# Column 0 of h in the second half: from twelve plain products per token tile to the rounds of seven block products

## The chip, the cores and the metric

The kernel runs on one core of one Trainium2 chip. The metric is the device time of one execution in microseconds (us); lower is better. TensorE (PE in the profile; PEld is its weight loading) multiplies, VectorE (DVE) and ScalarE (ACT) work elementwise, and nearly all transfers are issued one after the other on SyncE's DMA queue (SP, SPq).

## The reference

```python
def _A_ref(x, w_r, w_i):                     # x: 2048 tokens x 576
    X = rfft2(x, axes=(-2, -1)) * (w_r + 1j * w_i)
    return irfft2(X, s=(S, D), axes=(-2, -1))

def _B_ref(x, w_gate, w_up, w_down):         # F = 4608
    h = sigmoid(x @ w_gate) * (x @ w_up)     # 2048 x 4608
    return h @ w_down                        # 2048 x 576

xn = layernorm(x)
return x + _A_ref(xn, A_w_r, A_w_i) + _B_ref(xn, B_w_gate, B_w_up, B_w_down)
```

All is float32. The kernel keeps that accuracy by splitting each factor into a high and a low part in TensorE's rounded format, so that one product of two numbers becomes three passes (high x high, high x low, low x high).

## The kernel before

**Halves, units, columns.** The 2048 tokens are done in two halves of 1024 (p = 0, 1), each as two chunks of 512 (c = 0, 1). The 4608 columns of h come in 36 blocks of 128. Unit u = 36p + f computes block f of h for the half p. Its matmuls into the banks pA, pB and pE (L710) are 128x512, seven to a product. The first two units of a half are "plain" (four products per chunk), all others are made of seven block products, that is 49 matmuls; product 0 of a unit is put already among the products of the unit before. ScalarE and VectorE make h from the banks (L803 to L836). Two units make a column j of h, 18 columns to a half.

**h times w_down, in two ways.** `down` (L840, matmuls at L860) takes one column and one tile of 128 tokens: 2 units x 3 passes x 2 halves of the output = 12 matmuls of 128x288 into po, then one addition to acc (L869). Eight tiles make a half, so a column costs 96 matmuls. `seven` (matmuls at L1071, bank ps) takes two columns and the whole half at once, as a 2x2 block product in seven items (`ITEMS`, `ROUND`): each item needs one sum of blocks of h (`factor`: the sum at L985, split into high and low on ScalarE at L989 and VectorE at L992) and one sum of blocks of w_down (for example T1 = B12 - B11), and has two steps of 12 matmuls of 128x288, each followed by one addition at L1005. A pair of columns costs 7 x 2 x 12 = 168 matmuls, a column alone 84. `seven` starts in the unit after the first pair is complete and makes one step behind each product of the units (`next(rounds)` in `beside`). In a "slow" pair the low part of the next item is made at its second step, otherwise at its first.

**Which columns go which way.** `SEVEN` holds columns 1 to 15. The first half pairs 2 to 15 (column 1 is done by `down`); the second half pairs [1,2], [3,4] ... [13,14] and does 15 alone. Columns 0, 16 and 17 go by `down` in both halves. `pend` holds the calls of `down` that are due, `spots` says behind which product of a unit one is put; those of column 0 of the second half lie in units 38 and 39.

**The weights of the second half.** In the first half the split blocks of w_gate and w_up go to DRAM (wsp) and come back in the second as 320 KB pieces (`get_w`, L323), seven pairs of pieces to a unit. The sums of w_down for the rounds lie in DRAM as fsp, split; an item of the second half loads its own from there (L968). The sums of the first half's pairs are made on the fly (`load_raw_d`, `sums_d` and `sub_d` at L930, `split_item` at L941). Column 1, paired only in the second half, has its sums made in the opening by `make_t` (L363). Column 0's split rows go to DRAM in the opening (wdsp) and are loaded once more for the second half (`load_rows_of`, L911).

**The middle.** The half ends with `down` for columns 16 and 17. As each tile of column 17 is added (L869), its acc is stored (`spill`, L872), and right behind that store `new_acc(1, m)` loads the rows of x that start the acc of the second half (L395). All these stand in program order on the one SP queue, so an issue that waits for its data holds those behind it. From unit 39 on the Fourier part of the result ("phase 1b", tiles 0 to 15; L502 to L543) is mixed into the units by a list of steps: its first matmul group is pd0 (L527, with cf, fh, fl), made from xs by eo (L510, L511), fh (L514, ScalarE) and fl (L515).

Of the kernel before, what the change touches and what calls it, by code (L numbers as in the profile page):

```python
# [13 lines left out]
OP = mybir.AluOpType  # L14
# [22 lines left out]
LATE = 2 * G  # L37
SEVEN = range(1, NF // G - 2)

TWOS = ([list(SEVEN[i:i + 2]) for i in range(1, len(SEVEN), 2)], [list(SEVEN[i:i + 2]) for i in range(0, len(SEVEN), 2)])  # L40
SLOTS = 10
# [122 lines left out]
def spectral_glu_kernel(ctx: ExitStack, tc: tile.TileContext, x, xt, xg, ri, w_in, w_down, out):  # L164
# [3 lines left out]
    def f32(ap):  # L168
        return ap.bitcast(F32)
# [173 lines left out]
    def parts_d(f):  # L343
        j, g = divmod(f, G)
        st, w = STD[j][:, g], flat(new_f((0, j, g), f"wd{f}"))
        placed(nc.scalar.activation(w[:, 0], st, AF.Copy))
        yield
        nc.vector.tensor_tensor(w[:, 1], st, f32(w[:, 0]), op=OP.subtract)
        if j not in SEVEN:
            nc.sync.dma_start(wdsp[f], f32(w).rearrange("p a d -> p (a d)"))  # L350
        else:
            for b in range(2):
                if (g, b) != (0, 1):
                    nc.sync.dma_start(fsp[j][:, WHERE[f"B{g + 1}{b + 1}"]], f32(w[:, :, b * HD:(b + 1) * HD]))
        yield

    def make_d(f, n):
# [3 lines left out]
        yield from parts_d(f)  # L361

    def make_t(j):  # L363

        b = STD[j].rearrange("p g (b d) -> p (g b) d", b=2)
        t = R["pool"].tile([P, 4, HD], F32, tag="xa", name=f"wt{j}", bufs=TPC)
        nc.vector.tensor_tensor(t[:, 1:3], b[:, 1::2], b[:, :2], op=OP.subtract)
        yield
        nc.vector.tensor_tensor(t[:, 3], b[:, 3], t[:, 1], op=OP.subtract)
        nc.vector.tensor_tensor(t[:, 0], b[:, 2], t[:, 3], op=OP.subtract)  # L370
        yield
        th, tl = (R["pool"].tile([P, 4, HD], F32R, tag="xa", name=f"{k}{j}", bufs=TPC) for k in ("wth", "wtl"))
        nc.scalar.activation(th, t, AF.Copy)
        yield
        nc.vector.tensor_tensor(tl, t, f32(th), op=OP.subtract)
        for i, v in enumerate((th, tl)):
            nc.sync.dma_start(fsp[j][:, WHERE["T4"]:WHERE["T4"] + 4, i], f32(v))
        yield

    def make_dt(j):  # L380

        yield
        yield
        for g in range(G):
            load_d(G * j + g)
        for _ in range(3):
            yield
        for g in range(G):
            yield from parts_d(G * j + g)
        if j in SEVEN:  # L390
            yield from make_t(j)

# [338 lines left out]
    def plain_ends(u, c, G_, bank):  # L731
        ends.append(lambda: nc.vector.tensor_tensor(place(u, c), G_, bank[1], op=OP.mult))
        ends.extend(parting(u, c))

# [108 lines left out]
    def down(p, j, m, together=True):  # L843
# [18 lines left out]
        def add():  # L862
            a = acc[t].rearrange("p (b d) -> p b d", b=2)
            if not together:
                for b in range(2):
                    nc.vector.tensor_tensor(a[:, b], a[:, b], pd[b], op=OP.add)
                    (nc.sync, nc.scalar)[b].dma_start(out[t, :, b * HD:(b + 1) * HD], a[:, b])
                return
            nc.vector.tensor_tensor(a, a, po[:, :, :HD], op=OP.add)  # L869
            if j == NF // G - 1:  # L870
                if p == 0:
                    nc.sync.dma_start(spill[m * P:(m + 1) * P, :], acc[t])  # L872
                    new_acc(1, m)
                else:
                    for i in range(2):
                        (nc.sync, nc.scalar)[i].dma_start(out[t, i * N1:(i + 1) * N1], acc[t][i * N1:(i + 1) * N1, :])
# [48 lines left out]
    def d(js, nm):  # L925
        return DT["d"][:, :len(js), POS[js[0], nm]]
# [27 lines left out]
    def split_rows(j, g):  # L954
# [6 lines left out]
        nc.vector.tensor_tensor(w[:, 1], src, f32(w[:, 0]), op=OP.subtract)  # L961
        nc.sync.dma_start(wdsp[G * j + g].rearrange("p (a b d) -> p a b d", a=2, b=2), f32(w))

    def load_item(n):
# [50 lines left out]
    def seven(p):  # L1015
# [8 lines left out]

        last = TWOS[p][-1] if p == 0 else TWOS[p][-2]
        if p == 0:
# [33 lines left out]
        for i, (n, mm) in enumerate(steps):  # L1060
# [6 lines left out]
            for s in range(2):  # L1067
                m = slice((2 * mm + s) * P, (2 * mm + s + 1) * P)
                parts_ = [(g, a, b) for g in range(len(js)) for a, b in ((0, 0), (0, 1), (1, 0))]
                for q, (g, a, b) in enumerate(parts_):  # L1070
                    nc.tensor.matmul(pd[:, s], h[:, g, a, m], w[:, g, b], start=q == 0 and not seeded,  # L1071
                                     stop=q == len(parts_) - 1, skip_group_check=seeded)
            slow = len(js) == 2 and js is not last
            if mm == 0:
# [339 lines left out]
    for e, p in ((NF, 0), (LAST, 1)):  # L1414
        j = NF // G - 2
        rows = load_rows_of if p else lambda p, j, g: split_rows(j, g)
        for u, i, *todo in ((e - 3, 5, (rows, p, j, 0)) if p else (e - 2, -1, (rows, p, j, 0)),
# [8 lines left out]
            extra.setdefault((u, i), []).extend(lambda a=a: a[0](*a[1:]) for a in todo)  # L1426

    def turn(n):

# [14 lines left out]
    for p in range(PAIRS):  # L1444

        calls = [(0, 0), (1, 0), (0, 1), (1, 1)] if p == 0 else [(0, 0), (0, 1), (1, 0), (1, 1)]
        for n, (f, c) in enumerate(calls):
            u = p * NF + f
            if p == 0 and n == 2:
                sides += [make_d(0, 2), make_d(1, 2)]  # L1450
            elif p and n == 2:
                for g in range(G):
                    load_rows_of(1, 0, g)
            if p == 0 and n < 2:
# [29 lines left out]
        late_input[0] = False  # L1484
        pend = [(p, 0, m) for m in range(0 if p else TPC, TPP)]

        for f in range(G, NF):
# [15 lines left out]
            spots = {i: 1 for i in (range(5) if f % G else range(4, 7))}  # L1503
            if u == NF + G:

                spots = {3: 2, 4: 2, 5: 2, 6: 2}
            elif f == NF - 2:
                spots = {i: 1 for i in range(2, 7)}
# [74 lines left out]
```

## Time and profile before

| | |
|---|---|
| three runs, median (lowest to highest) | 1371.35 us (1370.74 to 1372.51) |
| the profiled execution: its time; its span | 1371.23 us; 1369.4 us |
| PE busy | 1356.5 us, 99% of the span, 7656 matmuls |
| PEld busy | 1200.8 us, 88% |
| DVE, ACT busy | 1068.6 us (78%), 775.5 us (57%) |
| moved by DMA | 346.56 MB, mean 253 GB/s |
| granted TensorE clock | 1.000 |

The span runs from the first to the last instruction on the core; the profiled execution's time lies 1.83 us above it. Busy times overlap, since the engines work at the same time. TensorE's matmuls are pipelined, so a single one's duration (391 ns for 128x512) is longer than the distance to the next; groups in the timeline show the distance. In the windows the columns are us, then busy time and count of PE, PEld, DVE, ACT and POOL, the granted clock, the share of the 16 DMA engines and GB/s.

### The profile page before, as it was taken

Reading aid. Unit: us, or ns where it says so; the run is one execution under the profiler, and the core shown is the slowest. Engines: PE = TensorE matmul, PEld = TensorE weight load, DVE = VectorE, ACT = ScalarE, POOL = GpSimd, SP = SyncE. Lnnn points to the kernel's source line nnn. Section 1 sums busy time; section 2 is a strip of 40 time slices with the busy share of each in tenths; the row PEclk is TensorE's granted clock in tenths of the full one; section 3 lists DMA queues with packets and bytes.
Section 4 is the critical chain, followed back from the end, with each engine's and each line's share of the span. In section 5 each row is a group of like instructions: output and inputs, shape, how many; then the busy total and the mean of one; then the engine's idle time right before and its main releaser. Section 6 shows DMA issues by size and latency. Waiting matters only on the chain.

```text
span 1369.4 us, 20371 instructions
## 1 busy us (share of the span) xinstructions
PE 1356.5 (99%) x7656; PEld 1200.8 (88%) x7656; DVE 1068.6 (78%) x1555; ACT 775.5 (57%) x1228; POOL 3.3 (0%) x5
## 2 busy tenths in 40 slices
PE   8999999999999999999999999999999999999998
PEld 6888888888888888988888998988888888899887
DVE  7978988887878787999458768668777847777886
ACT  6644667676777677843236545447767634443432
POOL 0000000000000000000000000000000000000000
PEclk9999999999999999999999999999999999999999
DMA  7567877767676776595878877799899787775643
GB/s 259 209 227 279 302 291 267 275 265 271 265 267 263 277 264 261 213 312 182 295 247 263 272 244 251 215 312 307 299 314 304 243 285 247 232 235 175 200 147 87
DMA packets 127058, 346.56 MB, mean 253 GB/s; under 512 B 12816, under 2 KB 34096, under 8 KB 122224
## 3 DMA queue, kind: packets, MB, share of 16 engines
q1 hardware_dynamic: 125968, 343.94, 72.5%
q8 instruction: 61, 1.00, 0.3%
q10 hardware_dynamic: 992, 1.31, 0.3%
q14 instruction: 37, 0.30, 0.1%
HBM read 208.74 MB, written 136.46 MB: 252 GB/s over the span
## 4 chain that ended last, share of the span: by engine, by line
PE 92%; DVE 5%; DMA 1%; ACT 1%; issue 1%; SPq 0%; ACTq 0%
PE pB L710 24%; PE ps L1071 23%; PE pE L710 16%; PE pA L710 16%; PE po L860 5%; PE pd L527 2%; PE pe L650 1%; PE pc L591 1%; PE py L619 1%; PE pa L543 1%; DMA w<-wsp 1%; PE pb L566 1%; PE pz L632 0%; DVE acc L869 0%; DVE X L1359 0%
## 5 line engine op out<-in xcount | busy, mean ns | idle before, releaser
L710 PE MATMUL pB<-X,w 128*128 128x512 f32 x1484 | 374.7, 391 | 0.1
L1071 PE MATMUL ps<-wf,hs 128*128 128x288 f32 x2436 | 358.4, 295 | 0.9 <-DVE ev L655 0.9
L1071 PEld LDWEIGHTS ps<-wf,hs 128*128 128x128 f32 x2436 | 341.7, 188 | 15.4 <-ACT u L593 1.9
L710 PEld LDWEIGHTS pB<-X,w 128*128 128x128 f32 x1484 | 270.9, 188 | 49.2 <-DVE X L477 0.6
L710 PE MATMUL pE<-X,w 128*128 128x512 f32 x1064 | 265.3, 391 | 1.7 <-DVE ys L834 1.0
L710 PE MATMUL pA<-X,w 128*128 128x512 f32 (+1 forms) x1006 | 252.8, 389 | 0.7 <-DVE X L1359 0.3
L710 PEld LDWEIGHTS pE<-X,w 128*128 128x128 f32 x1064 | 194.1, 188 | 37.9 <-issue 1.4
L710 PEld LDWEIGHTS pA<-X,w 128*128 128x128 f32 x1006 | 182.5, 188 | 33.7 <-ACT X L476 0.7
L992 DVE TENSOR_TENSOR hs<-ys,hs 128x1024 fp32r<-128x1024 f32 (+1 forms) x105 | 124.7, 1187 | 36.3 <-ACT hs L989 35.0
L989 ACT ACTIVATE hs<-ys 128x1024 fp32r<-128x1024 f32 (+1 forms) x105 | 108.0, 1029 | 42.8 <-PE ps L1071 27.0
L282 ACT ACTIVATE w<-raw 128x768 fp32r<-128x768 f32 (+1 forms) x106 | 100.2, 948 | 25.7 <-DVE raw L306 8.6
L803 ACT ACTIVATE v<-pB 128x512 f32<-128x512 f32 x68 | 40.6, 596 | 79.9 <-PE pB L710 79.4
L836 DVE TENSOR_TENSOR ys<-ys,g 128x1024 f32<-128x1024 f32 x67 | 81.9, 1223 | 3.4 <-DVE ys L834 0.5
L284 DVE TENSOR_TENSOR w<-raw,w 128x512 fp32r<-128x512 f32 (+1 forms) x106 | 81.7, 771 | 2.9 <-ACT w L282 2.8
L817 ACT ACTIVATE g<-pB 128x512 f32<-128x512 f32 x68 | 40.7, 598 | 67.3 <-PE pB L710 67.0
L985 DVE TENSOR_TENSOR ys<-ys 128x1024 f32<-128x1024 f32 (+1 forms) x60 | 71.1, 1186 | 0.7
L860 PEld LDWEIGHTS po<-wb,hp 128*128 128x128 f32 x468 | 65.2, 188 | 3.0 <-DVE acc L869 0.4
L814 DVE TENSOR_TENSOR ys<-v,pE 128x512 f32<-128x512 f32 x68 | 46.5, 684 | 27.0 <-ACT v L809 26.6
L860 PE MATMUL po<-wb,hp 128*128 128x288 f32 x468 | 67.5, 296 | 0.0
L1005 DVE TENSOR_TENSOR acc<-acc,ps 128x576 f32<-128x576 f32 x55 | 41.3, 751 | 30.9 <-PE ps L1071 30.4
L834 DVE TENSOR_TENSOR ys<-v,pE 128x512 f32<-128x512 f32 x67 | 45.9, 685 | 22.8 <-PE pE L710 21.7
L869 DVE TENSOR_TENSOR acc<-acc,po 128x576 f32<-128x576 f32 x55 | 41.1, 751 | 24.4 <-PE po L860 24.2
(185 smaller groups left out, 1581.5 us busy)
## 6 DMA issues: line engine op xcount, KB each, us to landing
w<-wsp SPq DMA_DIRECT2D x246, 320.0 KB, 4.0
wsp<-w SPq DMA_DIRECT2D x34, 2240.0 KB, 6.8
wf<-fsp SPq DMA_DIRECT2D x105, 288.0 KB, 4.2
fsp<-wf SPq DMA_DIRECT2D x98, 288.0 KB, 3.5
raw<-in_w SPq DMA_DIRECT2D x34, 768.0 KB, 6.5
x<-sc SPq DMA_DIRECT2D x16, 580.0 KB, 5.4
ri<-in_ri SPq DMA_DIRECT2D x16, 580.0 KB, 5.8
dt<-in_wd SPq DMA_DIRECT2D x32, 288.0 KB, 5.1
```

The costliest lines, as they stand in the source:

```text
L282: placed(nc.scalar.activation(o[:, :, :3, :], src, AF.Copy))
L284: placed(nc.vector.tensor_tensor(o[:, :, 3:, :], src[:, :, :KT, :], f32(o[:, :, :KT, :]), op=OP.subtract))
L710: strictly(nc.tensor.matmul(bank[:, cols], w[:, sw, :], X[:, x, sx, cols], start=start and j == 0, stop=stop and j == len(steps) - 1, skip ...
L814: nc.vector.tensor_tensor(y1, v[:, 1], bank["E"], op=OP.add)
L834: nc.vector.tensor_tensor(place(u, 0), v[:, 0], bank["E"], op=OP.add)
L836: nc.vector.tensor_tensor(h, h, g, op=OP.mult)
L860: nc.tensor.matmul(pd[b], l, r, start=start, stop=stop)
L985: nc.vector.tensor_tensor(o, at(a), at(b), op=op)
L989: nc.scalar.activation(hs[:, :, 0], o, AF.Copy)
L992: nc.vector.tensor_tensor(hs[:, :, 1], o, f32(hs[:, :, 0]), op=OP.subtract)
L1005: nc.vector.tensor_tensor(o, a, b, op=op)
L1071: nc.tensor.matmul(pd[:, s], h[:, g, a, m], w[:, g, b], start=q == 0 and not seeded, stop=q == len(parts_) - 1, skip_group_check=seeded)
```

## The change

`SEVEN` begins with column 0. The first half's pairs stay [2,3] to [14,15]; the second half's become [0,1], [2,3] ... [14,15], eight full pairs and no single column. So in the second half column 0 is no longer done by `down`: its h isn't split on its own, its rows of w_down aren't loaded for it, and units 38 and 39 have no `down` in them. The rounds begin in unit 39 in place of unit 41.

The sums of w_down for the pair [0,1] (T1 to T4 of both columns) are made by a new generator, `first_sums`, which makes one move per product of the second half's plain units, from unit 37 on: four loads of 288 KB, four subtractions, four splits on ScalarE and VectorE, eight stores of 288 KB into fsp. `make_t`, which did this for column 1 in the opening, is gone. Column 0's split blocks B11, B21, B22 go into fsp in the opening, three stores of 288 KB in place of two of 576 KB. `new_acc(1, m)` moves from behind the spills to units 38 (m = 0 to 6) and 39 (m = 7).

```diff
-SEVEN = range(1, NF // G - 2)
-
-TWOS = ([list(SEVEN[i:i + 2]) for i in range(1, len(SEVEN), 2)], [list(SEVEN[i:i + 2]) for i in range(0, len(SEVEN), 2)])
+SEVEN = range(NF // G - 2)
+
+PAIRED = [list(SEVEN[i:i + 2]) for i in range(0, len(SEVEN), 2)]
+TWOS = (PAIRED[1:], PAIRED)
...
-    def make_t(j):
...
-        nc.vector.tensor_tensor(t[:, 1:3], b[:, 1::2], b[:, :2], op=OP.subtract)
...
-        nc.vector.tensor_tensor(t[:, 3], b[:, 3], t[:, 1], op=OP.subtract)
-        nc.vector.tensor_tensor(t[:, 0], b[:, 2], t[:, 3], op=OP.subtract)
...
-        nc.scalar.activation(th, t, AF.Copy)
...
-        nc.vector.tensor_tensor(tl, t, f32(th), op=OP.subtract)
-        for i, v in enumerate((th, tl)):
-            nc.sync.dma_start(fsp[j][:, WHERE["T4"]:WHERE["T4"] + 4, i], f32(v))
...
-        if j in SEVEN:
-            yield from make_t(j)
...
-        ends.extend(parting(u, c))
+        if u < NF:
+            ends.extend(parting(u, c))
...
                     nc.sync.dma_start(spill[m * P:(m + 1) * P, :], acc[t])
-                    new_acc(1, m)
...
+    def first_sums():
+
+        js = TWOS[1][0]
+        for _ in range(4):
+            yield
+        for g in range(G):
+            load_raw_d(js, g)
+            yield
+        yield
+        yield
+        for i in range(2):
+            sums_d(js, i)
+            yield
+        sub_d(js, "T4", "B21", "T2", "B11")
+        for nm in ("T4", "T1", "T3", "T2"):
+            w = new_f((1, nm), f"wt_{nm}")
+            nc.scalar.activation(w[:, :, 0], d(js, nm), AF.Copy)
+            nc.vector.tensor_tensor(w[:, :, 1], d(js, nm), f32(w[:, :, 0]), op=OP.subtract)
+            for i, j in enumerate(js):
+                nc.sync.dma_start(fsp[j][:, WHERE[nm]], f32(w[:, i]))
+            yield
...
-        last = TWOS[p][-1] if p == 0 else TWOS[p][-2]
+        last = TWOS[p][-1]
...
-            slow = len(js) == 2 and js is not last
+            slow = js is not last
...
+    for m in range(TPP):
+        extra.setdefault((NF + G + m // 7, m % 7), []).append(lambda m=m: new_acc(1, m))
...
             elif p and n == 2:
-                for g in range(G):
-                    load_rows_of(1, 0, g)
+                sides.append(first_sums())
...
-        pend = [(p, 0, m) for m in range(0 if p else TPC, TPP)]
+        assert not (p and pend)
+        pend = [] if p else [(p, 0, m) for m in range(TPC, TPP)]
...
-            if u == NF + G:
-
-                spots = {3: 2, 4: 2, 5: 2, 6: 2}
-            elif f == NF - 2:
+            if f == NF - 2:
```

In the changed file the lines between about 350 and 960 stand some 21 lower in number (L710 is L689 there, L860 is L840, L869 is L849).

**SP's queue in the middle.** Before, from the last spills to the first pieces of unit 39's weights (w38 is the buffer of units 38 and later, wsp2 and wsp3 the stored weights of units 38 and 39):

```order
L872 DMA spill_72<-acc_163 128x576 x3
L395 DMA acc_163<-in_x 128x576 x3
L911 DMA wb1_0_0_6040<-wdsp0_109 128x1152
L911 DMA wb1_0_1_6042<-wdsp1_110 128x1152
L323 DMA w38_6055<-wsp2_75 128x640 x6
L323 DMA w38_6055<-wsp3_76 128x640
L172 DMA cf_6353<-c_cf 128x2900
L323 DMA w38_6055<-wsp3_76 128x640 x4
L502 DMA xs0_6364<-in_xt 128x768
```

And now:

```order
L852 DMA spill_72<-acc_164 128x576
L324 DMA w38_6032<-wsp2_75 128x640 x4
L374 DMA acc_164<-in_x 128x576 x5
L324 DMA w38_6032<-wsp3_76 128x640
L964 DMA fsp0_145<-wt_T4_6168 128x576
L324 DMA w38_6032<-wsp3_76 128x640
L964 DMA fsp1_146<-wt_T4_6168 128x576
L324 DMA w38_6032<-wsp3_76 128x640 x2
L964 DMA fsp0_145<-wt_T1_6183 128x576
L964 DMA fsp1_146<-wt_T1_6183 128x576
```

Unit 38's pieces moved from behind the last acc loads and the two wb loads to between and right behind the spills, five acc loads moved behind them, the wb loads are gone, and stores of the new sums stand between the pieces of unit 39. The queue then goes on:

```order
L324 DMA w38_6032<-wsp3_76 128x640
L173 DMA cf_6247<-c_cf 128x2900
L324 DMA w38_6032<-wsp4_77 128x640
L481 DMA xs0_6258<-in_xt 128x768
L173 DMA am0_6260<-c_am 128x512
L324 DMA w38_6032<-wsp4_77 128x640 x4
```

Unit 40's first pieces (wsp4) stand behind all eight stores, the 1450 KB load of cf, xs0 and am0.

**TensorE, units 38 to 40.** Before, behind the last product into pA38:

```order
L710 MATMUL pA38_6143<-X_66,w38_6055 128x512 x7
L710 MATMUL pB38_6151<-X_66,w38_6055 128x512 x7
L860 MATMUL po0_8_6195<-wb1_0_0_6040,hp1_0_0_5951 128x288 x6
L860 MATMUL po0_8_6195<-wb1_0_1_6042,hp1_0_0_5951 128x288 x6
L860 MATMUL po0_9_6208<-wb1_0_0_6040,hp1_0_0_5951 128x288 x6
L860 MATMUL po0_9_6208<-wb1_0_1_6042,hp1_0_0_5951 128x288 x6
L710 MATMUL pA39_6224<-X_66,w38_6055 128x512 x7
```

And now, from the same place up to the first group of phase 1b:

```order
L689 MATMUL pB38_6127<-X_66,w38_6032 128x512 x7
L689 MATMUL pE38_6128<-X_66,w38_6032 128x512 x7
L689 MATMUL pE39_6231<-X_66,w38_6032 128x512 x7
L689 MATMUL pB39_6230<-X_66,w38_6032 128x512 x7
L689 MATMUL pA39_6188<-X_66,w38_6032 128x512 x7
L689 MATMUL pB39_6230<-X_66,w38_6032 128x512 x14
L689 MATMUL pE39_6231<-X_66,w38_6032 128x512 x7
L689 MATMUL pA40_6281<-X_66,w38_6032 128x512 x7
L689 MATMUL pE40_6332<-X_66,w38_6032 128x512 x7
L506 MATMUL pd0_6343<-cf_6247,fh0_6302 128x290
```

The products of units 38, 39 and 40 follow each other with no matmul of `down` between them.

**VectorE ahead of pd0.** Before:

```order
L814 TENSOR_TENSOR ys_173<-v39_6336,pE39_6338 128x512
L510 TENSOR_TENSOR eo0_6405<-xs0_6364 128x384
L515 TENSOR_TENSOR fl0_6409<-eo0_6405,fh0_6408 128x512
L517 TENSOR_TENSOR fh0_6408<-eo0_6405,fh0_6408 32x2x128
L511 TENSOR_TENSOR eo1_6483<-xs1_6413 128x384
L834 TENSOR_TENSOR ys_173<-v39_6336,pE39_6338 128x512
L836 TENSOR_TENSOR ys_173<-ys_173,g39_6335 128x2x512
```

And now:

```order
L814 TENSOR_TENSOR ys_174<-v39_6229,pE39_6231 128x512
L816 TENSOR_TENSOR ys_174<-ys_174,g39_6228 128x2x512
L489 TENSOR_TENSOR eo0_6299<-xs0_6258 128x384
L490 TENSOR_TENSOR eo0_6299<-xs0_6258 128x384
L995 TENSOR_TENSOR hs1_0_1_6384<-ys_174,hs1_0_1_6384 128x2x512
L494 TENSOR_TENSOR fl0_6303<-eo0_6299,fh0_6302 128x512
L496 TENSOR_TENSOR fh0_6302<-eo0_6299,fh0_6302 32x2x128
```

Both halves of eo0 now come behind the last work on unit 39's h (its second half of the product, and the multiplication at L816), and the low part of the rounds' second item (L995) stands ahead of fl0.

More of the change, by code (lines that the diff above doesn't have):

```diff
@@ L348, in parts_d @@
         nc.vector.tensor_tensor(w[:, 1], st, f32(w[:, 0]), op=OP.subtract)
[L349 to L354, printed above, removed]
+        for b in range(2):
+            if (g, b) != (0, 1):
+                nc.sync.dma_start(fsp[j][:, WHERE[f"B{g + 1}{b + 1}"]], f32(w[:, :, b * HD:(b + 1) * HD]))
         yield
@@ L361, in make_d @@
         yield from parts_d(f)
-    def make_t(j):
-        b = STD[j].rearrange("p g (b d) -> p (g b) d", b=2)
-        t = R["pool"].tile([P, 4, HD], F32, tag="xa", name=f"wt{j}", bufs=TPC)
-        nc.vector.tensor_tensor(t[:, 1:3], b[:, 1::2], b[:, :2], op=OP.subtract)
-        yield
-        nc.vector.tensor_tensor(t[:, 3], b[:, 3], t[:, 1], op=OP.subtract)
-        nc.vector.tensor_tensor(t[:, 0], b[:, 2], t[:, 3], op=OP.subtract)
-        yield
-        th, tl = (R["pool"].tile([P, 4, HD], F32R, tag="xa", name=f"{k}{j}", bufs=TPC) for k in ("wth", "wtl"))
-        nc.scalar.activation(th, t, AF.Copy)
-        yield
-        nc.vector.tensor_tensor(tl, t, f32(th), op=OP.subtract)
-        for i, v in enumerate((th, tl)):
-            nc.sync.dma_start(fsp[j][:, WHERE["T4"]:WHERE["T4"] + 4, i], f32(v))
-        yield
     def make_dt(j):
@@ L962, in split_rows @@
         nc.sync.dma_start(wdsp[G * j + g].rearrange("p (a b d) -> p a b d", a=2, b=2), f32(w))
+        if j == js[1]:
+            free_d.extend((a, b))
+    def first_sums():
[18 more added lines that the diff above has]
+            yield
     def load_item(n):
```

## The prediction

> **What bounds the kernel.** I read the busy shares first, then the chain of waits, then what TensorE waited for.
>
> ```profile
> PE 1356.5 (99%) x7656; PEld 1200.8 (88%) x7656; DVE 1068.6 (78%) x1555; ACT 775.5 (57%) x1228; POOL 3.3 (0%) x5
> 754.55 1.62 PE ps L1071 x12
> 1355.86 8.06 PE po L860 x60
> PE b L1147 <- DMA idr<-c_id: 3.9, 1, 3.9
> PE pE L710 <- DVE ys L834: 1.0, 1, 1.0
> PE ps L1071 <- DVE ev L655: 0.9, 2, 0.7
> PE pE L710 <- DMA w<-wsp: 0.7, 1, 0.7
> ```
>
> TensorE is busy 99% of the span, and the first row of the waits (3.9 us) is the start of the program. The other rows shown are 1.0, 0.9 and 0.7 us. So the kernel lasts as long as TensorE's list, and an edit is worth the matmuls it takes out, plus the waits it makes or removes. A matmul's price isn't its 296 ns duration but its distance to the next: the second row of the chain gives 12 matmuls of 128x288 in 1.62 us, 135 ns each, for the rounds, the third 60 in 8.06 us, 134 ns each, for `down`. The two kinds cost the same.
>
> **Term A, fewer matmuls: -1.6 us.** Removed are 8 tiles x 12 = 96 matmuls into po. The single column 15 (84) and the pairs [1,2] to [13,14] become eight pairs: 8 x 168 against 7 x 168 + 84, so 84 more into ps. Net 12 fewer, 12 x 134 ns = 1.6 us. This is the change's whole saving of work.
>
> ```profile
> L860 PE MATMUL po<-wb,hp 128*128 128x288 f32 x468 | 67.5, 296 | 0.0
> L860 PEld LDWEIGHTS po<-wb,hp 128*128 128x128 f32 x468 | 65.2, 188 | 3.0 <-DVE acc L869 0.4
> ```
>
> The rows above show the weight loads of the same matmuls at 188 ns. The Trainium skill (Perfetto Trace Analysis, Identifying the Most-Contended Engine) judges TensorE by its weight loads' busy share, not by the matmuls'; read so, the 12 would be worth 12 x 188 ns = 2.3 us and the sum 0.7 us lower. The chain disagrees: 60 loads of 188 ns would be 11.3 us, and those 60 pairs took 8.06.
>
> **Term B, unit 38's late weights: -0.7 us.**
>
> ```profile
> 652.97 1.77 SPq L395 DMA_DIRECT2D acc<-in_x  x3
> 654.84 0.86 SPq L911 DMA_DIRECT2D wb<-wdsp  x2
> 655.75 8.38 SPq L323 DMA_DIRECT2D w<-wsp  x7
> 664.23 0.38 SPq L172 DMA_DIRECT2D cf<-c_cf  x1
> 666.37 5.09 SPq L323 DMA_DIRECT2D w<-wsp  x4
> 655.75 8.60 DMA w<-wsp
> 662.03 1.75 PE L710 MATMUL pA<-X,w 128*128 128x512 f32 x7
> 664.48 1.86 PE L710 MATMUL pE<-X,w 128*128 128x512 f32 x7 [0.70 <-DMA w<-wsp]
> 666.18 1.76 PE L710 MATMUL pB<-X,w 128*128 128x512 f32 x7
> ```
>
> The first five rows are SP's queue: six of unit 38's seven pieces were issued only from 655.75, behind acc loads that waited for spills and behind two wb loads. The sixth row is the chain: the piece took 8.60 us to land. The rest is TensorE: the group at 662.03 should be followed after 1.61 us, at 663.6, but the next began at 664.48. In the new queue the pieces stand right behind the spills, five acc loads come later and no wb load is there, so they land some 5 us sooner than needed. The wait itself is 0.70, the gap 0.87; I take -0.7 (0 if another piece is late, -0.9 at best). A stall that goes can come back at the next late transfer, and that is term C.
>
> **Term C, units 38 to 40 without their cover: +1.0 us (0 to 5).** Before, 8 x 1.6 = 12.8 us of `down` stood between the products of units 38 and 39. Now the products run back to back. With the wait gone, pE38 starts at 663.6; from it unit 40's second product (pE40) is the fifteenth, and starts at 663.6 + 14 x 1.61 = 686.1; pd0 follows at 687.8. Two things must be there.
>
> First, unit 40's weights. Its second piece stands on the queue behind seven pieces of unit 39, eight stores of new sums, cf, one piece of unit 40, xs0 and am0.
>
> ```profile
> w<-wsp SPq DMA_DIRECT2D x246, 320.0 KB, 4.0
> fsp<-wf SPq DMA_DIRECT2D x98, 288.0 KB, 3.5
> cf<-c_cf SPq DMA_DIRECT2D x1, 1450.0 KB, 8.6
> xs<-in_xt SPq DMA_DIRECT2D x16, 384.0 KB, 4.6
> am<-c_am SPq DMA_DIRECT2D x16, 256.0 KB, 3.5
> 660.00:670.00 10.00, 9.30 (x41) 7.41 (x40) 3.89 (x5) 3.96 (x7) 0.00 (x0) 1.00 1.02 400
> 710.00:720.00 10.00, 10.00 (x53) 8.38 (x52) 7.34 (x13) 5.35 (x10) 0.00 (x0) 1.00 0.92 286
> ```
>
> Up to and with that piece it is 9 x 320 + 8 x 288 + 1450 + 384 + 256 = 7274 KB, 7.45 MB, none of it sooner than 663.6, when pA38 lets go of the first buffer. At the 400 GB/s of the window from 660 (DMA share 1.02, so full) it takes 18.6 us; with about 2 us more until the last is seen, an estimate from half of the 4.0 us that a piece takes from issue to landing, it is there at 684.2: just in time. At the 286 GB/s of the window from 710, whose share is 0.92, it takes 26.0 us, to 691.6: 5.5 us late. I take 0 for this wait, since the queue is full here as at 660, where the rate was 400. The Trainium skill (SBUF — State Buffer, Summary: rules for kernel authors) says to reckon about 358 GB/s between HBM and SBUF; by it the piece comes at 686.4, and the sum would be 0.3 us higher. The 400 of the window above stands against it as a ceiling.
>
> Second, pd0's inputs fh and fl.
>
> ```profile
> L510 DVE TENSOR_TENSOR eo<-xs 128x384 f32<-128x384 f32 x16 | 8.9, 556 | 0.3
> L514 ACT ACTIVATE fh<-eo 128x768 fp32r<-128x768 f32 x16 | 13.5, 843 | 8.0 <-DVE eo L510 7.6
> L515 DVE TENSOR_TENSOR fl<-eo,fh 128x512 fp32r<-128x512 f32 x16 | 11.1, 691 | 6.7 <-ACT fh L514 6.7
> L834 DVE TENSOR_TENSOR ys<-v,pE 128x512 f32<-128x512 f32 x67 | 45.9, 685 | 22.8 <-PE pE L710 21.7
> L836 DVE TENSOR_TENSOR ys<-ys,g 128x1024 f32<-128x1024 f32 x67 | 81.9, 1223 | 3.4 <-DVE ys L834 0.5
> L992 DVE TENSOR_TENSOR hs<-ys,hs 128x1024 fp32r<-128x1024 f32 (+1 forms) x105 | 124.7, 1187 | 36.3 <-ACT hs L989 35.0
> 678.20 0.55 DVE L511 TENSOR_TENSOR eo<-xs 128x384 f32<-128x384 f32 x1
> ```
>
> One half of eo was made at 678.20 before (last row), some 23 us ahead of its use. VectorE works in order, and now both halves stand behind unit 39's last product, which ends at 684.5: then L834 0.69, L836 1.22, twice 0.56 for eo, to 687.5; then ScalarE's fh 0.84, to 688.4. TensorE wants fh at 687.8, and fl after L992 (1.19) and 0.69 more at about 689.4. I make it 1.0 us (0 if ScalarE's share is quick, 2 if its own queue is held by hs). If the weights are late by more, this wait lies inside that one, so C is the larger of the two.
>
> **Term D, the stretch where VectorE leads: +0.2 us (0 to 0.5).**
>
> ```profile
> 600.00:630.00 30.00, 29.70 (x164) 25.82 (x163) 29.73 (x34) 11.76 (x18) 0.00 (x0) 1.00 0.64 230
> 630.00:640.00 10.00, 8.97 (x52) 7.64 (x51) 9.69 (x13) 3.22 (x5) 0.00 (x0) 1.00 0.49 178
> 650.00:660.00 10.00, 10.00 (x46) 8.27 (x45) 5.49 (x7) 3.51 (x6) 0.00 (x0) 1.00 0.84 287
> 1224.00:1269.00 45.00, 44.81 (x284) 40.89 (x283) 33.24 (x50) 17.61 (x33) 0.00 (x0) 1.00 0.62 196
> ```
>
> From 600 to 640 VectorE has no idle time, and the 1.0 us wait for L834 is there. One load of 288 KB now comes ahead of this stretch's mr loads (0.72 us at 400 GB/s); what of that reaches TensorE I put at 0.2.
>
> **At nothing.**
> ```profile
> L930 DVE TENSOR_TENSOR dt<-dt 128x576 f32<-128x576 f32 x28 | 21.1, 755 | 0.4
> L941 DVE TENSOR_TENSOR wf<-dt,wf 128x576 fp32r<-128x576 f32 x49 | 36.9, 753 | 0.0
> ```
>
> The opening loses `make_t`, four operations of VectorE and two stores, where TensorE doesn't wait for VectorE in any row of the waits above. `first_sums` puts eight VectorE operations like these, of 0.76 us, between 650 and 668, where VectorE is busy 5.49 and 3.89 of 10 us, while the splits of column 0 and its eight additions go. Without that cover they would cost up to 6 us. At the end, two more pairs' quick steps: the window from 1224, where the last pair runs now, has TensorE at 44.81 of 45 us with VectorE at 33.24, so I expect 0, within 0.8.
>
> **Sum.** -1.6 - 0.7 + 1.0 + 0.2 = -1.1, so 1371.23 - 1.1 = 1370.1 for an execution like the profiled one. That one lies 0.12 below the median of the runs, so I predict **1370.2 us**, no change that can be measured: 0.2% is 2.7 us, about what a measurement of this kernel can tell from nothing.
>
> **Rivals.**
> - *The queue of units 38 to 40 is too slow* (slower). Mechanism as in C. For it: the window at 710 gives 286 GB/s, and eight of these transfers are stores mixed with loads. Against it: the share was 0.92 there, so the engines weren't full. At 286 the wait is 5.5 instead of 1.0: 1370.2 + 4.5 = 1374.7. It decides from the rate at which the sum reaches +2.7, a wait of 4.8 us: 7.45 MB in 25.3 us, 294 GB/s. I give it 0.10.
> - *No new wait, and the small ones shrink* (faster). pd0 is fed in time, D is 0, and the two waits for L655 (0.9 us) fall otherwise, since the rounds are shifted against the steps of phase 1b: -1.6 - 0.7 - 0.9 = -3.2, 1368.2. For it: those waits hang on the order in which short operations meet. Against: the order ahead of pd0 speaks plainly for a wait. I give it 0.18.
> - *The change gives up its 1.6 us in scattered waits* (no change). The rounds now run beside phase 1b from unit 39 on, two units sooner, and seven of their 56 items in this half grow from one column to two, with seven loads of 288 KB more. A wait of 0.2 us at some ten steps would bring 1371.4 to 1372.4. I give it 0.25, the forecast 0.47.
>
> **Range and chances.** The forecast's own range, 1369.0 to 1371.2, with the third case up to 1372.4 and the second down to 1368: 8 in 10 lie between 1367.9 and 1373.2. Faster than 1368.6: 0.20 (the second case and a rest of the forecast); slower than 1374.1: 0.11 (the first case); the same: 0.69.
>
> **What would show it.** Right: 12 matmuls fewer in the counts, with po at 8 tiles less; no wait of L710 for w<-wsp at 663; a wait of pd0 of about 1 us for fh or fl near 688; pE40 starting right behind pA40. Wrong: a wait for w<-wsp of several us near 686; waits of ps for L992 or for wf in the second half; a span that falls by more than the matmuls' 1.6 and the 0.7, or a stretch after 700 in which TensorE's idle time differs by more than 1 us from before.

## The result and the profile after

The changed kernel takes 1372.83 us (median of 18 runs), the kernel before 1371.07 (18 runs): 1.0015 times as long, 95% interval 1.0008 to 1.0022. That is slower by 1.8 us: less than the 0.2% that the forecast took for the least that can be told, but the interval is clear of 1. The forecast was 1370.2, so 0.9 us faster: inside the range (1367.9 to 1373.2), on the wrong side. One of the 18 runs took 1612.72 us at a granted clock of 0.778 and is left out of the ratio; without it the median is 1372.70.

The profiled execution took 1372.41 us with a span of 1369.9, against 1371.23 and 1369.4. The page of the changed kernel (busy shares, then the two groups of matmuls that were traded):

```profile
PE 1356.3 (99%) x7644; PEld 1200.0 (88%) x7644; DVE 1069.9 (78%) x1547; ACT 778.5 (57%) x1227; POOL 3.3 (0%) x5
L1074 PE MATMUL ps<-wf,hs 128*128 128x288 f32 x2520 | 370.0, 295 | 0.5 <-DVE acc L1008 0.2
L840 PE MATMUL po<-wb,hp 128*128 128x288 f32 x372 | 53.9, 296 | 0.0
```

The counts are those of term A: 84 more into ps, 96 fewer into po, 12 fewer in all. What TensorE waited for, without the start of the program:

```profile
PE pE L689 <- DVE ys L814: 1.2, 1, 1.2
PE pE L689 <- DMA w<-wsp: 1.0, 1, 1.0
PE pB L689 <- ACT v L789: 0.7, 1, 0.7
...
PE pd L506 <- DVE x1l L244: 0.4, 1, 0.4
```

The wait for w<-wsp is there again, but it is another one. TensorE's timeline from unit 38 to the first group of phase 1b:

```profile
661.89 1.75 PE L689 MATMUL pA<-X,w 128*128 128x512 f32 x7
663.47 1.75 PE L689 MATMUL pE<-X,w 128*128 128x512 f32 x7
...
679.68 1.75 PE L689 MATMUL pB<-X,w 128*128 128x512 f32 x7
682.12 1.88 PE L689 MATMUL pB<-X,w 128*128 128x512 f32 x7 [0.69 <-ACT v L789]
683.83 1.75 PE L689 MATMUL pE<-X,w 128*128 128x512 f32 x7
685.42 1.75 PE L689 MATMUL pA<-X,w 128*128 128x512 f32 x7
688.20 1.89 PE L689 MATMUL pE<-X,w 128*128 128x512 f32 x7 [1.03 <-DMA w<-wsp]
689.92 0.29 PE L506 MATMUL pd<-cf,fh 128*128 128x290 f32 x1
```

The old wait at 663 is gone: pE38 follows pA38 after 1.58 us (663.47 - 661.89), where it took 2.45. In its place stand a wait of pB for ScalarE's v at 682 and one for unit 40's second piece at 688. From pE38 to pd0 there are 15 products and nothing else; they took 689.92 - 663.47 = 26.45 us. This distance is the measure in all experiments below, since in the kernels where nothing is late it is 23.81.

The SP queue and the windows of the same stretch (the last two columns are the share of the DMA engines and GB/s):

```profile
663.67 0.33 SPq L324 DMA_DIRECT2D w<-wsp  x1
664.72 0.33 SPq L964 DMA_DIRECT2D fsp<-wt_T  x1
...
675.11 0.32 SPq L324 DMA_DIRECT2D w<-wsp  x1
675.48 1.08 SPq L173 DMA_DIRECT2D cf<-c_cf  x1
676.61 0.49 SPq L324 DMA_DIRECT2D w<-wsp  x1
...
678.43 3.35 SPq L324 DMA_DIRECT2D w<-wsp  x4
```

```profile
660.00:670.00 10.00, 10.00 (x46) 8.28 (x45) 4.60 (x6) 5.10 (x8) 0.00 (x0) 1.00 0.64 212
670.00:680.00 10.00, 9.95 (x44) 7.91 (x44) 4.49 (x5) 4.13 (x7) 0.00 (x0) 1.00 1.02 372
680.00:690.00 10.00, 8.29 (x36) 6.21 (x35) 4.69 (x7) 3.95 (x6) 0.00 (x0) 1.00 1.01 399
```

Up to 670 the engines were only 64% busy: each of unit 39's pieces has to wait until TensorE lets go of its buffer, one per product, and each pair of stores for its split. From 670 on they were full. Unit 40's second piece was issued at 678.43, the first of the group of four, behind all that had piled up, and TensorE went on only at 688.20.

### The profile page after: what moved, and what is told of

Same layout as the page of the kernel before. It is cut to its first block, busy times and chain, and to the rows that moved or that the text cites. A ratio compares the mean times of both kernels' runs of the same rounds, so it can differ in the third digit from the quotient of the medians.

```text
span 1369.9 us, 20335 instructions
## 1 busy us (share of the span) xinstructions
PE 1356.3 (99%) x7644; PEld 1200.0 (88%) x7644; DVE 1069.9 (78%) x1547; ACT 778.5 (57%) x1227; POOL 3.3 (0%) x5
## 5 line engine op out<-in xcount | busy, mean ns | idle before, releaser
L689 PE MATMUL pB<-X,w 128*128 128x512 f32 x1484 | 375.1, 391 | 0.9 <-ACT v L789 0.7
L1074 PE MATMUL ps<-wf,hs 128*128 128x288 f32 x2520 | 370.0, 295 | 0.5 <-DVE acc L1008 0.2
L1074 PEld LDWEIGHTS ps<-wf,hs 128*128 128x128 f32 x2520 | 353.2, 188 | 15.5 <-ACT u L572 1.9
L689 PEld LDWEIGHTS pB<-X,w 128*128 128x128 f32 x1484 | 270.9, 188 | 50.7 <-ACT v L789 1.8
L689 PE MATMUL pE<-X,w 128*128 128x512 f32 x1064 | 266.4, 391 | 2.2 <-DVE ys L814 1.2
L689 PE MATMUL pA<-X,w 128*128 128x512 f32 (+1 forms) x1006 | 252.9, 389 | 0.3 <-ACT X L455 0.3
L689 PEld LDWEIGHTS pE<-X,w 128*128 128x128 f32 x1064 | 194.1, 188 | 38.4 <-issue 1.6
L689 PEld LDWEIGHTS pA<-X,w 128*128 128x128 f32 x1006 | 182.5, 188 | 33.0 <-ACT X L455 0.7
L995 DVE TENSOR_TENSOR hs<-ys,hs 128x1024 fp32r<-128x1024 f32 x105 | 128.4, 1223 | 43.5 <-ACT hs L992 42.8
L992 ACT ACTIVATE hs<-ys 128x1024 fp32r<-128x1024 f32 x105 | 111.0, 1058 | 53.1 <-PE ps L1074 29.3
L816 DVE TENSOR_TENSOR ys<-ys,g 128x1024 f32<-128x1024 f32 x67 | 81.9, 1223 | 3.2
L783 ACT ACTIVATE v<-pB 128x512 f32<-128x512 f32 x68 | 40.5, 596 | 64.8 <-PE pB L689 64.4
L988 DVE TENSOR_TENSOR ys<-ys 128x1024 f32<-128x1024 f32 x60 | 73.2, 1221 | 0.7
L814 DVE TENSOR_TENSOR ys<-v,pE 128x512 f32<-128x512 f32 x67 | 45.9, 685 | 30.0 <-PE pE L689 28.8
L514 ACT ACTIVATE ah<-pd,rstd 64x290 fp32r<-64x290 f32 x64 | 31.9, 498 | 50.6 <-PE pd L506 33.5
L789 ACT ACTIVATE v<-pB 128x512 f32<-128x512 f32 x68 | 40.4, 595 | 32.8 <-PE pB L689 32.5
L515 DVE SCALAR_TENSOR_TENSOR al<-pd,rstd,ah 64x290 fp32r<-64x290 f32 x64 | 33.2, 519 | 32.2 <-ACT ah L514 31.3
```

The costliest lines, as they stand in the source:

```text
L689: strictly(nc.tensor.matmul(bank[:, cols], w[:, sw, :], X[:, x, sx, cols], start=start and j == 0, stop=stop and j == len(steps) - 1, skip ...
L814: nc.vector.tensor_tensor(place(u, 0), v[:, 0], bank["E"], op=OP.add)
L816: nc.vector.tensor_tensor(h, h, g, op=OP.mult)
L988: nc.vector.tensor_tensor(o, at(a), at(b), op=op)
L992: nc.scalar.activation(hs[:, :, 0], o, AF.Copy)
L995: nc.vector.tensor_tensor(hs[:, :, 1], o, f32(hs[:, :, 0]), op=OP.subtract)
```

## The experiments

**The changed kernel again, twice.** Both without an edit, 11 and 10 timed runs.

> The changed kernel once more, to see how its waits differ between two executions. Theory Q (the queue of units 38 to 40 is overfull: eight stores, cf and the weights): the wait of TensorE for unit 40's weight piece near 687 is there again, 0.5 to 3 us, together with the wait of pB for ScalarE's v near 681 (0.7 us), and TensorE's excess between 662 and 700 is 2.5 us or more; median 1372.8, 1.8 us over before. Rival L (the loss lies at the end, in the quick last pair between 1220 and 1300): the excess there differs between the executions, that between 662 and 700 doesn't.

Measured: 1373.27 us, 1.0016 times the kernel before (1.0008 to 1.0025). The wait of pB for v is the same 0.69, that for w<-wsp is 1.67, and from pE38 to pd0 it takes 27.17 us. Rival L fell: by the distances between matmuls that are added up further below, the end (1220 to 1298) loses the same in both executions to 0.1 us, while 662 to 700 loses 0.4 us more in this one.

> The changed kernel a third time: how far TensorE's wait for unit 40's piece and the whole span go together. Theory Q: the waits for w<-wsp near 687 of three executions (1.0, 1.7 and this one) and their spans rise together, and the median of the timed runs, 1 us above the profiled spans, is a longer wait of the same kind. Rival: a third execution with a longer span has the same wait and loses elsewhere.

Measured: 1372.95 us, 1.0015 (1.0006 to 1.0024). Here the weight piece was less late, and TensorE's timeline shows what takes over:

```profile
687.92 1.88 PE L689 MATMUL pE<-X,w 128*128 128x512 f32 x7 [0.35 <-DMA w<-wsp]
690.00 0.40 PE L506 MATMUL pd<-cf,fh 128*128 128x290 f32 x1 [0.20 <-ACT fh L493]
690.24 0.63 PE L689 MATMUL pB<-X,w 128*128 128x512 f32 x2
691.13 0.40 PE L506 MATMUL pd<-cf,fl 128*128 128x290 f32 x1 [0.27 <-DVE fl L494]
```

From pE38 to pd0 it is 26.07 us. So the three executions lose 2.6, 3.4 and 2.3 us against 23.81, and where the weights come sooner, fh and fl are next, as the prediction had it ("C is the larger of the two"). The expectation that the wait for w<-wsp and the span rise together fell: the execution with the smallest wait had the longest span (1370.4, against 1369.9 and 1370.1). The rival was right here: by the distances between matmuls this execution lost 0.5 to 0.6 us more than the other two in its first 50 us, far from the change. All three profiled spans lie below the medians of the timed runs' spans, 1370.7, 1371.1 and 1370.65, and which wait makes up that difference wasn't seen.

**Without the eight stores.**

```diff
             nc.vector.tensor_tensor(w[:, :, 1], d(js, nm), f32(w[:, :, 0]), op=OP.subtract)
-            for i, j in enumerate(js):
-                nc.sync.dma_start(fsp[j][:, WHERE[nm]], f32(w[:, i]))
             yield
```

> The changed kernel without the eight stores of the new weight sums (the rounds of the first pair then read another stored block in the place of T1 to T4, so the output is not the reference's); the sums themselves are still made. Theory Q: 2.4 MB leave the queue between 663 and 675, unit 40's weight piece lands 4 to 6 us sooner, its wait (1.0 us) is gone, the lead product of unit 40 stands again between the two products into pB and the wait for ScalarE's v (0.7 us) goes too: 2.0 us less than the changed kernel, 1370.8. Rival F (pd0's inputs fh and fl are as late as the weights): the wait moves to pd0, 0.5 us less at most, 1372.3. Rival L (the end): no change, 1372.8.

Measured: 1369.99 us, 0.9993 times the kernel before (0.9984 to 1.0002), 3.3 us less than the changed kernel in the same comparison. TensorE's timeline:

```profile
680.40 1.75 PE L689 MATMUL pB<-X,w 128*128 128x512 f32 x7
681.99 1.75 PE L689 MATMUL pA<-X,w 128*128 128x512 f32 x7
683.58 1.75 PE L689 MATMUL pB<-X,w 128*128 128x512 f32 x7
685.16 3.34 PE L689 MATMUL pE<-X,w 128*128 128x512 f32 x14
688.34 0.29 PE L506 MATMUL pd<-cf,fh 128*128 128x290 f32 x1
```

Neither wait is left, from pE38 to pd0 it takes 23.81 us, and the lead product of unit 40 (its product 0, put among unit 39's; pA at 681.99) stands between the two into pB. The rival that pd0's inputs would take over the wait fell too: xs0 comes sooner without the stores, so eo is made ahead of unit 39's last product. Not only the stores differ, though: the built program has another order, TensorE's as said, and on SP's queue cf is issued at 668.31, seven us sooner and ahead of unit 39's last pieces. The loss of the change goes with the stores on the queue, and the four loads, four subtractions and eight splits, which are all still made here, cost nothing that can be seen.

**Down between the products, and the stores.** The kernel before with eight stores of the same size.

```diff
+    def dummy(k):
+        nc.sync.dma_start(scratch[k], f32(HS[1, 0, 1]).rearrange("p g i t -> p (g i t)")[:, 1024:1024 + D])
+
+    for k in range(8):
+        extra.setdefault((NF + G, 1 + k // 2), []).append(lambda k=k: dummy(k))
```

> The kernel before, with its down products in units 38 and 39, and eight stores of 288 KB more at the place on the queue where the changed kernel has them (they write a part of h that was just made to an unused place in DRAM). Theory Q (the stores hurt because the products of units 38 to 40 lost the 12.8 us of down between them): unit 40's second piece lands some 6 us later than before but is wanted only at about 699, so no wait longer than 0.3 us appears, 1371.1. Rival S (eight stores between the weight loads cost by themselves, wherever they are): the wait for w<-wsp near 663 grows or a new one comes, 1 to 3 us, 1372 to 1374.

Measured: 1370.89 us, 0.9997 (0.9988 to 1.0005), so no change. The windows of 660 to 680 and two rows of TensorE's timeline:

```profile
660.00:670.00 10.00, 10.00 (x46) 8.23 (x45) 3.89 (x5) 4.21 (x7) 0.00 (x0) 1.00 1.02 395
670.00:680.00 10.00, 10.00 (x67) 9.37 (x66) 3.71 (x5) 0.73 (x2) 0.00 (x0) 1.00 1.01 400
```

```profile
662.12 1.75 PE L711 MATMUL pA<-X,w 128*128 128x512 f32 x7
663.71 1.77 PE L711 MATMUL pE<-X,w 128*128 128x512 f32 x7
```

The DMA engines are full for 20 us, as they are in the changed kernel from 670 on, and TensorE is never idle: with the 12.8 us of `down` between the products the stores are free. With the run above this makes the four corners of one square: stores without `down` cost some 3 us, each of the other three nothing. The last two rows bring a surprise for term B. Unit 38's weights are issued here as in the kernel before, and yet pE38 follows after 1.59 us: the wait of 0.70 that the prediction saw wasn't in this execution.

**Only the acc loads moved.** The kernel before with this part of the change alone:

```diff
                     nc.sync.dma_start(spill[m * P:(m + 1) * P, :], acc[t])
-                    new_acc(1, m)
...
+    for m in range(TPP):
+        extra.setdefault((NF + G, -1), []).append(lambda m=m: new_acc(1, m))
```

> The kernel before with one part of the change alone: the loads of the second half's acc are moved from behind each spill to unit 38. Term B of the prediction: unit 38's pieces are issued sooner, the wait of 0.7 us for w<-wsp at 663 goes, 0.9 us less than before, 1370.2. Rival: another piece or the acc loads are late instead, no change, 1371.1.

Measured: 1370.85 us, 0.9998 (0.9989 to 1.0007). In its profile the wait at 663 is gone. The gain of 0.25 us can't be told from nothing, and it is less than the 0.9 of the profiled execution. That fits a wait that only some executions have, but there is one profile of the kernel before, so it isn't shown.

**Four of the stores later.**

```diff
         for nm in ("T4", "T1", "T3", "T2"):
+            for _ in range({"T3": 6}.get(nm, 0)):
+                yield
```

> The changed kernel with the sums T3 and T2 made and stored six products later, so that four of the eight stores stand behind unit 40's first pieces on the queue; nothing else. Theory Q: 1.18 MB less ahead of unit 40's second piece, which lands 3 us sooner; its wait and that for ScalarE's v near 681 go, 2 to 3 us less than the changed kernel, 1370.0 to 1371.0. Rival M (the queue stays full, so the wait only moves to a later piece of unit 40 or 41): a wait of 1 us or more for w<-wsp after 690, 1372 to 1373.

Measured: 1372.76 us, 1.001 (1.0001 to 1.0018): nothing gained. TensorE's timeline:

```profile
680.05 1.75 PE L689 MATMUL pB<-X,w 128*128 128x512 f32 x7
683.00 1.86 PE L689 MATMUL pA<-X,w 128*128 128x512 f32 x7 [1.20 <-DMA w<-wsp]
...
698.79 0.37 PE L1076 MATMUL ps<-wf,hs 128*128 128x288 f32 x1 [0.87 <-DVE al L515]
```

The rival M was right that the wait moves, though to an earlier place: the lead product is back between the two into pB, so unit 40's first piece is wanted 3.8 us sooner (681.64, one product after the row at 680.05, in place of 685.42), and that one still stands behind cf. The second wait, 0.87 us at 698.79, is put down to VectorE; whether it was that or the item's own weights from fsp wasn't tried.

**The stores on another queue.**

```diff
-                nc.sync.dma_start(fsp[j][:, WHERE[nm]], f32(w[:, i]))
+                nc.scalar.dma_start(fsp[j][:, WHERE[nm]], f32(w[:, i]))
```

> The changed kernel with its eight new stores issued on ScalarE's DMA queue in place of SP's: the same bytes at the same time, but no longer ahead of the weight pieces on one queue (unit 40's first piece then also stands ahead of cf). Rival B (the bytes alone decide, since all queues share the 16 DMA engines): the pieces come as late as before, a wait for w<-wsp of 0.7 us or more between 680 and 690, 1372 to 1373. Theory O (the order on the one queue decides: the stores are not urgent and must not stand ahead): the pieces are 2 us or more sooner, no such wait over 0.3 us, 1370 to 1371. ScalarE's eight issues cost TensorE nothing by either.

Measured: 1372.59 us, 1.001 (1.0 to 1.0019). Two waits by kind, of the list of the whole execution:

```profile
PE pB L689 <- DMA w<-wsp: 1.7, 1, 1.7
...
PE ps L1074 <- DMA wf<-fsp: 0.5, 1, 0.5
```

And of SP's queue:

```profile
674.74 0.38 SPq L324 DMA_DIRECT2D w<-wsp  x1
675.17 0.42 SPq L173 DMA_DIRECT2D cf<-c_cf  x1
675.70 1.36 SPq L324 DMA_DIRECT2D w<-wsp  x2
```

No gain, as rival B had it, but the order on SP's queue isn't the expected one: cf now stands ahead of unit 39's last piece (the first of the two at 675.70), and that is the piece that is late. So the run doesn't compare the two queues alone. What it shows is that the same bytes in the same stretch cost about as much: from pE38 to pd0 it takes 25.88 us, 2.1 more than 23.81, and here without any wait of pB for v.

**Phase 1b a unit later.**

```diff
-U1, U2, U3 = (0, 4.1), (76, 4.1), (151, 4.5)
+U1, U2, U3 = (7, 3.6), (76, 4.1), (151, 4.5)
...
-    begin[0] = [stage1]
+    begin[U1[0]] = [stage1]
```

> The changed kernel with phase 1b begun one unit later (its tiles follow each other after 3.6 in place of 4.1 products, so that they end where they did): cf, xs0 and am0, 2.1 MB, leave the place ahead of unit 40's pieces, the eight stores stay. Theory Q (the sum of bytes ahead of the piece decides, not that they are stores): both waits go, 2 to 3 us less, 1370 to 1371, unless the denser phase 1b costs something after 700 (0 to 2 us). Rival S (stores are what is slow): the wait near 687 stays over 0.5 us, 1372 or more.

Measured: 1372.26 us, 1.0007 (0.9999 to 1.0016). The window of the crowded stretch:

```profile
680.00:690.00 10.00, 10.00 (x50) 8.25 (x49) 2.60 (x3) 3.42 (x5) 0.00 (x0) 1.00 0.95 324
```

TensorE is never idle there, with all eight stores in place: 2.1 MB less of anything ahead of the pieces is enough, so stores aren't slow as such. But the time fell by 0.6 us only, not by 2 to 3. The distances between matmuls show where most of the gain went: against the changed kernel's profiled execution this one loses 2.5 us less between 662 and 700 and 1.6 us more between 700 and 880, half of that between 760 and 800. The same stretch costs 1.0 us more in the run with both edits, further below, than in the one with the sums in the opening alone. So the denser phase 1b has a price of 1 to 1.6 us in the profiles, as the expectation allowed. The profiled execution, at 1371.06 us, was the fastest of the 11.

**The sums in the opening.** Column 0 still joins the rounds; T1 to T4 of both columns are made by `make_t`, as column 1's were before, and `first_sums` isn't used.

```diff
+    def make_both():
+        yield from make_t(0)
+        yield from make_dt(1)
...
-                sides.append(first_sums())
...
-                wd = make_dt(f // G)
+                wd = make_both()
```

> The changed kernel with the weight sums of columns 0 and 1 made in the opening, as the kernel before made those of column 1, and nothing made in the middle. Theory Q: the middle has neither the eight stores nor the four loads, so both waits near 681 and 687 go as in the run without stores, and the opening loses 0 to 0.5 us: 1370.7 to 1371.3. Rival O (the opening has no room on VectorE and the queue for a second set of sums): 1 to 3 us come back before 110 us, 1372 to 1374. Rival L: 1372.8.

Measured: 1370.13 us, 0.9995 (0.9986 to 1.0004), and in a second comparison:

> The run with the sums of columns 0 and 1 made in the opening once more, for its time against the kernel before: 1370.1, 1.0 us less than before by the first run; by the terms -1.6 (matmuls) and -0.5 to -0.9 (unit 38's pieces), +0.6 (the end) and +0.4 (around 865), 0 to -1 (700 to 760), it should be 0.5 to 1.7 us less.

Measured: 1369.93 us against 1370.93, 0.9994 (0.9985 to 1.0003). TensorE's timeline of the second, in which no product of units 38 to 40 waits:

```profile
681.16 1.75 PE L711 MATMUL pA<-X,w 128*128 128x512 f32 x7
682.75 1.75 PE L711 MATMUL pB<-X,w 128*128 128x512 f32 x7
684.33 3.34 PE L711 MATMUL pE<-X,w 128*128 128x512 f32 x14
687.51 0.29 PE L528 MATMUL pd<-cf,fh 128*128 128x290 f32 x1
```

Both times 1.0 us less than the kernel before and some 3 less than the changed one. Each interval reaches just over 1, so a gain over the kernel before is likely and not shown; the gain over the changed kernel is clear. The opening had room for a second set of sums.

**The same, with phase 1b a unit later too.** Both edits together.

> The changed kernel with the sums of columns 0 and 1 made in the opening, and with phase 1b one unit later too. If the bytes at 663 to 690 are the whole of it, the second step brings nothing on top of the first: the same as the run with the sums in the opening, 1370.1 within 0.5; what differs from it is the price of the denser phase 1b alone (0 to 2 us).

Measured: 1370.49 us, 0.9991 (0.9982 to 1.0). The second step brings nothing on top of the first; by the medians it costs 0.4 us (0.6 against the second run with the sums in the opening), within the 0 to 2 expected.

**The order of the lead product by itself.** The run with the sums in the opening, and TensorE's order around unit 39 held to that of the changed kernel:

```diff
+        strict[0] = strict[0] or u == NF + 3
...
-        if (u + 1) % NF:
+        if (u + 1) % NF and u != NF + 3:
             lead(u + 1)
...
         made(6)
+        if u == NF + 3:
+            lead(u + 1)
```

> The run with the sums in the opening, in which no weight piece is late, with TensorE's order around unit 39 forced to that of the changed kernel: the lead product of unit 40 (pA40) behind pE39, so that two products into pB stand back to back. If that order has a price of its own (the bank pB must be read by ScalarE for v before the second product may start), a wait of 0.7 us of pB for ScalarE's v at 680 comes back with no weight piece late, and the time rises by 0.8 us to 1370.8. Rival: the wait near 681 of the changed kernel was only the weights' lateness in another place; then it is not there and the time stays at 1370.0.

Measured: 1370.35 us, 0.9996 (0.9987 to 1.0005). TensorE's timeline:

```profile
679.70 1.75 PE L711 MATMUL pB<-X,w 128*128 128x512 f32 x7
682.14 1.88 PE L711 MATMUL pB<-X,w 128*128 128x512 f32 x7 [0.69 <-ACT v L814]
683.86 1.75 PE L711 MATMUL pE<-X,w 128*128 128x512 f32 x7
```

The wait came back to the hundredth, with no piece late, so it is the price of the order: two products into one bank back to back, 2.44 us from start to start in place of 1.59. From pE38 to pd0 it takes 24.79 us, 1.0 more than 23.81. The time rose by 0.2 to 0.4 us only, of 0.8 expected, and the interval can't tell these.

## Why the prediction was wrong

**A (-1.6 us): the count held.** The kernels that do the rounds' work of the change with nothing late (without stores, and with the sums in the opening) have median spans of 1368.0, against 1369.3 before: -1.3. That fits -1.6, but the small terms below are in it too, and no run takes the twelve matmuls out alone.

**B (-0.7 us) held in the profiled execution and not in the mean.** There the gap closed by 0.87 us (2.45 to 1.58). Alone it brought 0.25 us that can't be told from nothing, and the kernel before with the extra stores didn't have the wait. I took one execution's DMA wait for a constant.

**C (+1.0 us) is the step that failed.** The stretch was right. But C was priced by the wait for pd0's inputs, with unit 40's weights in time; it was the weights that were late, and C came to 2.3 to 3.4.

The failed step is "I take 0 for this wait, since the queue is full here as at 660". I let 7.45 MB start at 663.6 and run at 400 GB/s, 18.6 us and 2 more until they are seen, to 684.2. In the changed kernel they took 24.6, and pE40 started when its piece came, at 688.20. With nothing late it would have started 14 products of 1.59 us behind pE38, at 685.7. Two windows of that stretch:

```profile
663.60:670.00 6.40, 6.40 (x30) 5.31 (x29) 2.40 (x4) 2.00 (x4) 0.00 (x0) 1.00 0.74 231
663.60:688.20 24.60, 22.84 (x100) 17.93 (x98) 10.05 (x14) 8.74 (x15) 0.00 (x0) 1.00 0.94 344
```

Until 670 the engines moved only 231 GB/s: the pieces of unit 39 come free one per product, and the stores wait for their splits. Against 400 GB/s that is 2.7 us. The 372 GB/s from 670 to 680 are 0.7 more. Over the whole stretch 8.46 MB were moved, 1.0 more than the 7.45: transfers issued behind the piece went beside it, 2.5 us of the engines' time, for which the forecast had its 2 us. So the main error was the idle start and not the rate. The 358 GB/s of the Trainium skill (SBUF — State Buffer, Summary: rules for kernel authors) was passed whenever the queue was full, at 372 and 399. With it the prediction puts the piece at 686.4 and its sum 0.3 us higher; by its own rule that C is the larger of the two waits, C would have stayed at 1.0.

The sum should have been made for the part behind the last of the issues that wait. From unit 39's last piece (675.11) on, 3.1 MB had to pass up to and with unit 40's second piece. By the landings in the trace, four stores and a piece of unit 39 that were issued before, 1.5 MB, were still on their way. Without these it is 7.8 us at 400 GB/s and 2 more, 684.9, in time again; with them 11.6 and 2 more, 688.7 (an estimate from these numbers), near the 688.20 measured.

The waits of pB for v weren't in the sum either. The one at 682 (0.85 us from start to start) stood in the order that was quoted: "pB39 x14", with pA40 behind pE39. I counted products and not the bank between them. Here, however, it cost nothing of its own: pE40 couldn't start before its piece came, so the wait lies inside that one, and the run with the stores on ScalarE's queue loses 2.1 us without it. `down` had not hidden it before, for all eight calls lay in unit 38; in unit 39 the lead product stood between the two into pB (at 693.30, 694.88 and 696.47). Why the built order of the changed kernel differs isn't shown. The small one at 671 (0.2 us) is another matter, since there a product into pA stands between. A split of the new sums was in ScalarE's way, itself held by a store:

```profile
670.39 0.69 ACT L961 ACTIVATE wt_T<-dt 128x576 fp32r<-128x576 f32 x1 [1.36 <-DMA fsp<-wt_T]
670.98 0.58 ACT L789 ACTIVATE v<-pB 128x512 f32<-128x512 f32 x1
```

pd0's inputs were placed about right: in one execution of three TensorE waited 0.20 and 0.27 us for fh and fl behind the weights' wait; in the other two pd0 began right behind pE40.

The rival that I gave 0.10, the slow queue of units 38 to 40, was nearest: late weights, but by the idle start and not by a rate of 286 GB/s. It cost 1.3 to 2.4 us more than forecast, not 4.5. The "no change that can be measured" was wrong too, since the interval tells 0.15% from nothing.

**D (+0.2) and the terms at nothing.** To see them, I took for every matmul the distance to the next less the usual distance of its shape in the kernel before, and added this up by stretch (us):

```
stretch     before   changed   sums in the opening (2nd)
600-640      2.20      2.20      2.54
662-700      1.11      3.11      0.40
700-760      1.28      0.29      0.65
800-880      1.01      1.43      1.48
940-1220     2.68      2.76      2.71
1220-1298    0.64      1.25      1.35
```

D was nothing: 2.20 both times, with the wait for L814 at 1.2 in place of 1.0 and a smaller one gone. 1.0 us of small waits went out of 700 to 760 (0.6 with the sums in the opening), a gain as the second rival had it, in another place; that the rounds running two units sooner are the cause wasn't tried. 0.4 us came up at 865 (pd for x1l, 0.4 in the waits above), and the quick last pair costs 0.6 us, inside the 0 within 0.8 that was said. So -1.6 of work, +2.0 at 662 to 700 (-0.9 for B in this execution, +2.9 for C and what follows it within pd0), -1.0, +0.4 and +0.6 make +0.4, against a span that grew by 0.5.

**What is left open.** Of what the timed runs moved by, 1.4 us lie in the span (medians 1369.3, from a later comparison, and 1370.7) and 0.3 around it: 1.78 us before, 2.06 in the changed kernel and 2.1 with the sums in the opening. No trace shows that stretch. And the medians of the timed runs' spans lie 0.25 to 1.0 us above the profiled ones of the changed kernel; the traces don't show by what.

## What to carry to other kernels

Work that looks like waste beside a critical queue can be its cover: the twelve matmuls saved were worth 1.6 us, and the 12.8 us of `down` that went with them had been hiding a burst of transfers. Before matmuls are taken out from between dependent products, sum the transfers that the next products want from the last issue that has to wait for a buffer, not from the first, and add what was issued before and hasn't landed. Look in the new order for two groups into one PSUM bank with nothing between them, and ask whether their wait lies inside a longer one. If a burst doesn't fit, move bytes out of the window (here to the opening); moving some of them to another queue or a little later in the same window only moved the wait.

## What the runs showed of the hardware

- Eight stores of 288 KB issued on ScalarE's queue in place of SP's didn't free the weight loads: with the DMA engines full from 670 to 690, TensorE still waited 1.7 us for a piece, where the three executions with one queue had 0.35 to 1.67. The order of the loads on SP's queue differed too.
- Two products into one PSUM bank with one ScalarE read of 128x512 between them (0.60 us) start 2.44 us apart, in place of 1.59 with other work between: 0.85 us, the same to 0.01 in four executions.
- The 15 products from pE38 to pd0 took 23.81 us in three different executions in which nothing was late, to the hundredth; in three executions of the changed kernel, in which a weight load was late, they took 26.07 to 27.17. In one comparison the 33 runs of the kernel before took from 1370.46 to 1371.88 us, the 11 of the changed kernel from 1372.17 to 1374.59.
